# Linear attention and gated MLP, two layers: key weights folded on TensorE for all tiles, and a new order of instructions

## Chip, cores, metric

One core of one Trainium2 chip. The metric is the device time of one execution in microseconds (us), median of several runs. Ratios are the mean time of one kernel's fast runs over that of the kernel before in the same rounds, with a 95% interval; so they are not quite the ratio of the medians quoted beside them.

## The reference, cut to what matters

The input has 2048 rows of 512 (bf16). Two layers, each an attention block and an MLP block, each on a layer-normalised copy with a residual sum. There are 32 heads of 16 features.

```
qkv   = x @ wqkv
pq,pk = per head:  q @ w_phi[h],  k @ w_phi[h]
phi   = concat(softmax(p), softmax(-p))          # for q and k: "two signs"
kv    = sum over all rows of phi_k^T v ;  z = sum over all rows of phi_k
o     = (phi_q @ kv) / (phi_q @ z + 1e-6) ;      x += o @ wo
mlp:    x += (relu(x @ W_gate) * (x @ W_up)) @ W_down
```

The sum over all rows is a barrier: no query product with `kv` can start before the last tile of 128 rows has given its keys.

## The kernel before, the parts that matter

The program makes some 2,100 operations, each for one engine, with a priority (`DUE`), and plans one order from them. Some operations can run on two engines; a string of bits (`PLACE`) chooses. The planned order is then emitted once, so each engine executes a fixed sequence.

The key projection and w_phi are folded into one weight, Wk2 = wk @ blockdiag(w_phi). For that wk must be transposed. Before, the DMA transposes it from HBM, and because that comes late, tiles 0 and 1 take a detour ("unfolded": project, copy, multiply by the block-diagonal).

```python
def fold(w, dst, loaded, due, step, engs, by_dma=False):
    wT = Buf(p_wT)
    for m in range(NB):                       # NB = 4 blocks
        if by_dma:
            ... nc.sync.dma_start_transpose(out=wT..., in_=w[m*P:(m+1)*P, :])   # "wT"
            continue
        ps = Buf(p_b)                         # this branch was there, unused
        tr = op("PE", ... 4 x nc.tensor.matmul(ps..., lhsT=w[:, m, b*P:(b+1)*P], rhs=ident) ...)   # "turn"
        turned.append(evac(engs[m % 2], ... ps -> wT ...))
    for m in range(NB):
        f = op("PE", ... 4 x matmul(ps..., lhsT=wT.t[:, b, m*P:(m+1)*P], rhs=Wblk[:, b, :]) ...)   # "fold"
        done.append(evac(engs[m % 2], ... ps -> dst[:, m, :] ...))                                 # "W2"
...
k_fold = fold(A_wqkv[:, D:2 * D], Wk2, None, 10, 3000, ("ACT", "DVE"), True)
q_fold = fold(A_wqkv[:, 0:D], Wq2, None, ..., ("ACT", "DVE"), True)
...
# per tile t, layer 0 and 1 (cut):
k  = K products (4 matmuls of 512 columns), or keys_unfolded for t < UNFOLDED
ek = exp(+k), exp(-k)                                    # ScalarE, 2 x 512 columns
v  = V products, copied to vext                          # ScalarE or VectorE
sk = sum of each head of ek                              # VectorE, 1024 columns
lnk, rk = ln(sk), exp(-ln)                               # ScalarE
phi = ek * rk                                            # two halves, GpSimd or VectorE
kvz: sums += phi^T [v, 1]                                # TensorE
...
# after the last tile: R = block-diagonal of the sums, sign by sign (VectorE), then the query products
```

The softmax here doesn't subtract the row's maximum and nothing guards it: scores larger than these inputs give would overflow.

## Time and profile before

| | kernel before |
|---|---|
| median of 6 runs | 387.62 us (387.31 to 388.71) |
| span in the profile | 385.5 us, granted clock 1.000 |
| first folded key product | 16.86 us |
| first block-diagonal sum R | 55.27 us |
| first MLP product | 66.84 us |
| TensorE busy, of it fillers up to 15.1 us | 374.3 us, 6.26 us |

How to read it: up to R the kernel makes keys and values for 16 tiles and fits the queries in; this I call the key phase. From R on TensorE is busy nearly without a gap to the end. So the time of R and of the first MLP product tell whether the start got shorter, and the rest can be compared on its own. Two rows of instruction groups on VectorE, from the start of the kernel before to 54.9 us, become important later (columns: group, count, busy us, mean ns of one, idle before):

```profile
L665 DVE TENSOR_SCALAR xn<-X,mvA,rsA 128x512 bf16<-128x512 bf16 x16 | 6.7, 441 | 0.6 <-ACT rsA L660 0.6
L722 DVE TENSOR_TENSOR phiK<-ek,sk 128x512 bf16<-128x512 bf16 x9 | 6.6, 772 | 0.0
```

### The profile page before, as it was taken

What the parts mean: (1) busy time and instruction counts of PE and PEld (TensorE: products, weight loads), DVE (VectorE), ACT (ScalarE), POOL (GpSimd) and SP (SyncE); (2) the same over time, 40 slices, a digit from 0 to 9 for tenths busy, and PEclk for the clock granted to TensorE, in tenths of its full rate; (3) what the DMA queues carried; (4) which work ended last, traced back from release to release, by engine and by line L of the source; (5) the groups of instructions that cost most, each with busy time, mean ns of one, the idle gap of its engine ahead of it and who ended that gap; (6) DMA issues with size and microseconds to landing.
All of it is one profiled execution on the core that took longest, in us unless ns stands there. A gap on an engine that the chain in (4) does not pass through costs nothing.

```text
span 385.5 us, 7662 instructions
## 1 busy us (share of the span) xinstructions
PE 374.3 (97%) x2811; PEld 225.8 (59%) x2857; DVE 312.8 (81%) x793; ACT 216.5 (56%) x555; POOL 39.4 (10%) x42
## 2 busy tenths in 40 slices
PE   8999998999999999999999999999999999999996
PEld 3545455877655544455667645596774445445875
DVE  5999999999999988557985697999997699663434
ACT  4899999645457536256365489983345412421421
POOL 0266820000010203010012201000000000000000
PEclk9999999999999999999999999999999999999999
DMA  9787640143224141011101000014234023211110
GB/s 233 113 248 209 166 131 2 37 70 62 43 55 70 27 84 27 14 30 34 29 14 36 15 1 0 3 32 66 56 70 98 14 42 83 41 16 61 32 32 27
DMA packets 63046, 23.36 MB, mean 61 GB/s; under 512 B 54849, under 2 KB 61985, under 8 KB 63009
## 3 DMA queue, kind: packets, MB, share of 16 engines
q1 hardware_dynamic: 62592, 22.48, 26.6%
q8 instruction: 22, 0.36, 0.4%
q10 hardware_dynamic: 416, 0.39, 0.4%
q14 instruction: 16, 0.12, 0.1%
HBM read 7.91 MB, written 2.10 MB: 26 GB/s over the span
## 4 chain that ended last, share of the span: by engine, by line
PE 71%; DVE 17%; ACT 5%; DMA 3%; issue 3%; SPq 0%; DVEq 0%; ACTq 0%
PE b L894 31%; PE b L927 18%; PE b L830 5%; PE b L780 4%; PE b L698 4%; PE b L692 3%; PE q L798 3%; DVE sk L703 2%; PE b L870 2%; DVE bstA L650 2%; DMA xnTA<-xn 2%; PE q L739 1%; DVE xn L665 1%; DMA X<-in_A_x_dram 1%; DVE hT L902 1%
## 5 line engine op out<-in xcount | busy, mean ns | idle before, releaser
L894 PE MATMUL b<-xnTB,wgu 128*128 128x128 bf16 (+2 forms) x1192 | 152.0, 279 | 1.2 <-ACT xnTB L590 0.8
L894 PEld LDWEIGHTS <-wgu 128*128 128x128 bf16 x1200 | 98.0, 98 | 45.6 <-issue 1.0
L898 ACT ACTIVATE gu<-b 128x512 bf16<-128x512 f32 (+1 forms) x83 | 48.0, 583 | 66.4 <-PE b L894 62.8
L927 PE MATMUL b<-wd,hT 128*128 128x512 bf16 (+2 forms) x347 | 84.4, 372 | 0.9
L722 POOL TENSOR_TENSOR phiK<-ek,sk 128x512 bf16<-128x512 bf16 x36 | 38.7, 1094 | 192.8 <-ACT sk L713 121.7
L902 DVE TENSOR_TENSOR hT<-gu 128x512 bf16<-128x512 bf16 (+1 forms) x83 | 34.6, 417 | 24.9 <-ACT gu L590 23.9
L927 PEld LDWEIGHTS <-hT 128*128 128x128 bf16 (+1 forms) x363 | 34.0, 98 | 31.8 <-DVE hT L902 1.1
L695 ACT ACTIVATE ek<-b 128x512 bf16<-128x512 f32 x64 | 36.1, 607 | 10.3 <-PE b L692 10.3
L703 DVE TENSOR_REDUCE sk<-ek 128x64 f32<-128x1024 bf16 x32 | 38.5, 1209 | 3.7 <-ACT ek L695 3.4
L590 ACT CAST gu<-b 128x512 bf16<-128x512 f32 (+1 forms) x51 | 29.1, 570 | 20.0 <-PE b L894 19.7
L784 ACT ACTIVATE Eq<-b 128x512 bf16<-128x512 f32 x64 | 36.3, 631 | 0.4 <-PE b L780 0.2
L934 DVE SCALAR_TENSOR_TENSOR X<-b,rsB,X 128x512 bf16<-128x512 f32 (+1 forms) x33 | 23.6, 727 | 11.6 <-PE b L927 11.4
L830 PE MATMUL b<-wo,oT 128*128 128x512 bf16 x121 | 32.2, 379 | 0.7 <-ACT oT L590 0.2
L698 PE MATMUL b<-wv,xnTA 128*128 128x512 bf16 x125 | 32.0, 379 | 0.2
L590 ACT CAST N<-q 128x384 bf16<-128x384 f32 (+1 forms) x58 | 25.0, 452 | 12.2 <-PE q L798 10.6
L780 PE MATMUL b<-xnTA,Wq 128*128 128x512 bf16 x124 | 31.1, 379 | 0.2
L692 PE MATMUL b<-Wk,xnTA 128*128 128x512 bf16 x114 | 29.8, 379 | 0.7 <-DMA xnTA<-xn 0.4
L798 PE MATMUL q<-R,Eq 128*128 128x144 bf16 x256 | 27.7, 226 | 0.7 <-DVE R L761 0.3
L591 DVE CAST gu<-b 128x512 bf16<-128x512 f32 (+1 forms) x32 | 21.5, 676 | 7.7 <-PE b L894 7.5
L798 PEld LDWEIGHTS <-Eq 128*128 128x128 bf16 x256 | 20.2, 98 | 10.3 <-issue 2.1
L650 DVE BATCH_NORM_STATS2 bstA<-X 128x6 f32<-128x512 bf16 x32 | 21.4, 684 | 3.4 <-DMA X<-in_A_x_dram 3.2
L834 DVE TENSOR_TENSOR X<-X,b 128x512 bf16<-128x512 bf16 x32 | 21.6, 676 | 2.0 <-PE b L830 2.0
(70 smaller groups left out, 395.5 us busy)
## 6 DMA issues: line engine op xcount, KB each, us to landing
out_dram<-X SPq DMA_DIRECT2D x15, 128.0 KB, 1.7
X<-in_A_x_dram SPq DMA_DIRECT2D x6, 256.0 KB, 3.7
wgu<-in_B_W_gate_dram SPq DMA_DIRECT2D x4, 344.0 KB, 4.0
wgu<-in_B_W_up_dram SPq DMA_DIRECT2D x4, 344.0 KB, 3.5
wd<-in_B_W_down_dram SPq DMA_DIRECT2D x5, 256.0 KB, 3.9
wv<-in_A_wqkv_dram SPq DMA_DIRECT2D x2, 256.0 KB, 5.0
wo<-in_A_wo_dram SPq DMA_DIRECT2D x4, 128.0 KB, 2.8
oT<-o SPq DMA_TRANSPOSE x28, 2.4
```

Of the source, the lines that this page charges most:

```text
L590: both = {"ACT": ("ACT", act(cols), lambda: nc.scalar.copy(out=out_(), in_=in_()), False), "DVE": ("DVE", dve(cols), lambda: nc.vector.ten ...
L692: k = op("PE", mm(4, 512), due, lambda: [nc.tensor.matmul(kp.t[:], lhsT=xnTA[c][:, b, cols], rhs=Wk2[:, b, :], start=(b == 0), stop=(b == ...
L698: v = op("PE", mm(4, 512), due_v, lambda: [nc.tensor.matmul(vp.t[:], lhsT=xnTA[c][:, b, cols], rhs=wv[:, b, :], start=(b == 0), stop=(b == ...
L703: a = op("DVE", SUM16, due, lambda: nc.vector.tensor_reduce(out=sk.t[:, row, :], in_=ek.t[:].rearrange("p g s (h f) -> p (g s h) f", f=DH) ...
L722: e.tensor_tensor(out=ph.t[:].rearrange("p g s (h f) -> p (g s h) f", f=DH)[:, lo:lo + n], in0=ek.t[:].rearrange("p g s (h f) -> p (g s h) ...
L780: q = op("PE", mm(4, 512), due(c, b), lambda b=b, qp=qp: [nc.tensor.matmul(qp.t[:], lhsT=Wq2[:, m, b * P:(b + 1) * P], rhs=xnTA[c][:, m, : ...
L798: pe.append(op("PE", mm(len(groups), GE), due, lambda ps=ps, groups=groups: [nc.tensor.matmul(ps.t[:, n * GE:(n + 1) * GE], lhsT=Eq[c][:, ...
L830: a = op("PE", mm(4, 512), due + 3, lambda: [nc.tensor.matmul(yp.t[:], lhsT=oT.t[:, b, :], rhs=wo[:, b, :], start=(b == 0), stop=(b == NB ...
L894: nc.tensor.matmul(ps.t[:, q * W:(q + 1) * W], lhsT=wgu[:, s, b, g * P:(g + 1) * P], rhs=xT.t[:, b, 0:W], start=(b == 0), stop=(b == NB - 1))
L898: nc.scalar.activation(out=gu.t[:, 0, 0:cols], in_=gp.t[:, 0:cols], func=AF.Relu)
L902: nc.vector.tensor_tensor(out=h.t[:, f0 * W:f0 * W + cols], in0=gu.t[:, 0, 0:cols], in1=gu.t[:, 1, 0:cols], op=Alu.mult)
L927: nc.tensor.matmul(yp.t[:, 0:c1 - c0], lhsT=h.t[:m, f * W + i * P:f * W + (i + 1) * P], rhs=wd[:m, f, c0:c1], start=(f == 0), stop=(f == N ...
```

## The change

Intent: have the folded keys earlier by turning wk on TensorE, from the copy that is on chip anyway, and drop the detour. Priorities and placement are new for the whole program.

```diff
-UNFOLDED = 2
-PLACE = ( ... 299 bits ... )        DUE = ( ... 2105 priorities ... )
+PLACE = ( ... 301 bits ... )        DUE = ( ... 2105 priorities ... )
-    k_fold = fold(A_wqkv[:, D:2 * D], Wk2, None, 10, 3000, ("ACT", "DVE"), True)
-    def keys_unfolded(t, kp, xT, due):
-        ... 16 matmuls of 128 columns, a copy, 4 matmuls of 128 columns ...
+    k_fold = fold(wk, Wk2, l_wk, 100, 100, ("ACT", "DVE"))
...
-            if self.l == 0 and t < UNFOLDED:
-                k = keys_unfolded(t, kp, xT, due)
-            else:
-                k = op("PE", mm(4, 512), due, ... K products with Wk2 ...)
+            k = op("PE", mm(4, 512), due, ... K products with Wk2 ...)
```

## The prediction

> **What bounds the kernel now.** I read the page first, then the busy time of each engine in stretches, then the first 20 us in order of time, and the chain of waits last. The page's first part:
>
> ```profile
> PE 374.3 (97%) x2811; PEld 225.8 (59%) x2857; DVE 312.8 (81%) x793; ACT 216.5 (56%) x555; POOL 39.4 (10%) x42
> ```
>
> TensorE is busy for 97% of a 385.5 us span, so any gain has to come from time in which it is idle or does work that the result doesn't need. Fillers (matmuls on a tile of zeros, line 584) are such work. The stretches show where both lie; columns are the stretch, its length, then busy us and instruction count of each engine:
>
> ```profile
> 0.00:6.00 6.00, 4.13 (x16) 1.65 (x17) 3.26 (x16) 1.86 (x4) 0.70 (x6) 1.00 0.69 199
> 6.00:15.10 9.10, 8.27 (x82) 5.03 (x82) 7.31 (x20) 6.50 (x19) 0.00 (x0) 1.00 0.93 201
> 15.10:57.00 41.90, 41.16 (x312) 21.20 (x315) 40.57 (x70) 39.85 (x109) 24.59 (x23) 1.00 0.71 181
> 57.00:67.00 10.00, 8.50 (x69) 5.02 (x70) 9.16 (x30) 9.99 (x31) 0.00 (x0) 1.00 0.01 2
> 240.00:251.00 11.00, 10.24 (x84) 6.16 (x84) 10.08 (x33) 10.75 (x31) 0.00 (x0) 1.00 0.01 2
> 251.00:380.00 129.00, 128.21 (x1004) 82.02 (x1017) 95.34 (x274) 49.12 (x112) 0.00 (x0) 1.00 0.23 48
> ```
>
> The reader is to see four things. In the first 15.1 us TensorE looks busy, but 3.90 + 2.36 = 6.26 us of its 12.40 us are fillers (same stretches, filler line alone). From 15.1 to 57 us, the keys and values of layer 0 with the queries fitted in, TensorE (41.2 of 41.9), VectorE (40.6) and ScalarE (39.9) are all full; only GpSimd has room (24.6). At 57 to 67 and 240 to 251 us, where attention begins in each layer, TensorE loses 1.5 and 0.8 us. Elsewhere it loses under 1%.
>
> Why is so little real work done before 15 us? The folded key weights come late:
>
> ```profile
> 5.32 10.94 SPq L600 DMA_TRANSPOSE hT<-in_A_wqkv_dram  x8
> 10.99 1.07 ACT L590 CAST Wk<-b 128x512 bf16<-128x512 f32 x2
> 12.98 0.67 DVE L591 CAST Wk<-b 128x512 bf16<-128x512 f32 x1
> 16.33 0.67 DVE L591 CAST Wk<-b 128x512 bf16<-128x512 f32 x1
> 16.37 1.19 SPq L638 DMA_TRANSPOSE xnTA<-xn  x1
> 16.86 1.03 PE L692 MATMUL b<-Wk,xnTA 128*128 128x512 bf16 x4
> ```
>
> Eight weight transposes (four for keys, four for queries) hold the issuing queue from 5.32 to 16.26 us; the fourth block of folded keys is copied at 16.33 us, and the first folded key product runs at 16.86. The detour for tiles 0 and 1 bridges this. Of the chain to 62 us, 10.7% is the key sum (VectorE, line 703), 10.0% the waits for transposes of activations, 8.4% query products: no single engine, but VectorE comes first.
>
> **What the Trainium skill says.** "DMA: Bandwidth & Descriptors", section "Alternative transpose paths", lists TensorE as the way to transpose data that is already on chip, with an identity, from SBUF into PSUM. That fits: the weight wk is on chip anyway. "TensorE: Matmul & The Clock Gate", Part 4, adds the price, a copy out of PSUM afterwards. The kernel here uses plain matmuls on the identity; the trace has four of them in 0.40 us (line 641) and the copy in about 0.59 us on ScalarE or 0.68 us on VectorE. "VectorE: DVE Perf Modes", section "Why PSUM operands drop a tier", says that an fp32 operand in PSUM holds VectorE to its single-rate mode; the trace agrees, since a 512-column copy out of PSUM takes 685 ns against 415 ns for the 512-column SBUF sum of line 826. So each added turn costs more on the copying engine than on TensorE. The main skill page, "Trainium Kernel Development and Optimization", section "Best Practices", warns not to judge the distance to roofline by matmul busy time; the 6.26 us of fillers are a case of it.
>
> **The change, part by part.** The short description names attention sums built sign by sign; the diff doesn't touch that code, which already loops over signs in the kernel before, so it is worth 0. Three parts remain.
>
> *Key fold on TensorE.* Removed: four DMA transposes of about 1.27 us of queue time each, 5.1 us in all. Added: 16 matmuls of 128 columns, 4 x 0.22 = 0.9 us of TensorE, and four copies of 0.6 to 0.7 us, 2.5 us together. When are folded keys ready? The two halves of wk were issued at 0.7 and 1.2 us with 3.4 and 3.7 us to landing: 4.1 and 4.9 us. The turns can follow at once. The block-diagonal w_phi is ready at 5.34 + 0.69 = 6.03 us. Four folds and four copies on two engines, beside the first xn copy, take about 2.3 us: complete near 8.3 us, an estimate, against 16.95 us now. That is 8.6 us earlier, and the queue is 5.1 us freer for tiles 4 and up.
>
> *No unfolded keys.* Removed: 32 matmuls of 128 columns (16 in about 0.87 us at the pace of the trace, so 1.7), 8 more (0.4), two ScalarE copies (1.2). Added: 8 matmuls of 512 columns (2 x 0.86 = 1.7). TensorE over both parts: +0.9 + 1.7 - 2.1 = +0.5 us, no saving. Tile 0 gets its keys at about the same time (8.3 now), but tile 1, whose exponentials now start at 15.57 us, and tiles 2 and 3 can go as soon as their x is there (7.8 to 9.8 us).
>
> *New placement string and order.* These come with the diff and re-decide the whole order. I matched the placement bits to the operations in the order in which the program makes them; for the kernel before this gives nine VectorE and 23 GpSimd phi halves in layer 0, as the trace has them. The new string gives, in the key phase of layer 0: VectorE two turn copies more (+1.4), one fold copy less (-0.7), one value copy less (-0.7), two phi halves more (+1.4): +1.4 us. ScalarE: two turn copies, one fold copy and one value copy more, two copies less: +1.2 us. GpSimd two halves less.
>
> **The sum.** TensorE alone could gain much: before 15.1 us it does 12.40 - 6.26 = 6.1 us of real work now and could do about 9.5 (turns and folds 1.7, four tiles of K and V 6.9, turns of xn 0.9), 3.4 us more, less the 0.5 added: 2.9 us. But the keys must also pass VectorE, which is full from 7.8 us on. Its work there changes by -1.4 (two key-fold copies, one of them gone, the other early) - 0.7 (value copy) + 1.4 (phi) = -0.7 us; the two turn copies fit into its hole between 6.03 and 7.82 us. Its holes later, 0.24, 0.51 and 0.44 us, can close in part. So the sums R, begun at 55.27 us now, should begin 0.7 to 1.9 us earlier, about 1.3. TensorE, ahead with its queries by then, waits for that. As it is bound from there on, this carries to the end nearly whole. I add 0.4 us for idle time that a new order may take off the two attention starts (2.3 us in all): 387.55 - 1.3 - 0.4 = 385.85, said as 385.8 us.
>
> **The rivals.** *TensorE sets the start, and the gain is the 2.9 us or more.* For it: it is full from 15.1 us on and its lead is real; ScalarE is idle for over 3 us between 5 and 15 us and could take VectorE's work. Against: the new string gives VectorE more, not less. Time: about 384. *The start is hidden and nothing comes of it.* VectorE has the same keys to sum (16 x 1.2 us), a new copy falls on the statistics of tiles 1 to 3, and TensorE merely idles later, near 55 us, instead of filling early. For it: VectorE at 40.6 of 41.9 us. Against: the small holes that do go away. Time: 387 to 388. *The new order hurts elsewhere.* The new string moves six of the 512-column copies of the up-projection and four value copies of layer 1 from ScalarE to VectorE in layer 0's main part, where VectorE is full in 100 to 130 us already. Against: it has slack from 140 to 240 us, and three phi halves go the other way. Time: 388 to 390.
>
> **Range and chances.** The work of TensorE hardly changes, and all that isn't its needed work is the 6 us of fillers and some 8 us of idle time up to 380 us, so over 2% (7.75 us, under 379.8) would need most of that: 0.03. Slower by over 2% needs a new wait of 8 us in a tuned order: 0.02. Within 2%: 0.95. The first rival's 384 with some luck gives the low end, 383.5; a wash with a slightly worse order the high end, 387.9.
>
> **What would show it right or wrong.** In the changed profile: four weight transposes instead of eight, and 16 matmuls with wk before 6 us; folded keys complete at 8 to 9 us and a first line of their product by 9.5 us, not 16.9; fewer fillers than the 6.3 us now; more real TensorE work before 15 us by 2 to 4 us; VectorE still full from about 8 us to the first R, and this R 0.7 to 1.9 us earlier; from R to the end the same length within 1 us. I am wrong in the mechanism if R comes 3 us earlier (VectorE was no bound), if it doesn't move while TensorE idles more before it, or if the difference arises after 67 us, where I have only the new order to blame.

## The result and the profile after

The changed kernel takes 386.5 us (386.07 to 386.79, 6 runs) against 387.62 us; ratio 0.9967 (0.9954 to 0.9981). That is 1.1 us faster, a real but small gain, within 2%.

The same stretches of the changed kernel (columns as in the prediction: stretch, length, busy us and count of TensorE, its weight loads, VectorE, ScalarE, GpSimd; then clock, DMA share, GB/s):

```profile
0.00:6.00 6.00, 4.74 (x21) 2.54 (x22) 3.45 (x17) 2.37 (x4) 0.70 (x6) 1.00 0.75 207
6.00:15.10 9.10, 8.48 (x76) 5.44 (x74) 8.66 (x20) 7.74 (x21) 0.00 (x0) 1.00 0.60 155
15.10:57.00 41.90, 41.54 (x307) 21.09 (x306) 40.41 (x74) 40.23 (x110) 22.66 (x21) 1.00 0.70 177
57.00:67.00 10.00, 8.36 (x84) 5.37 (x82) 9.45 (x31) 9.29 (x30) 0.00 (x0) 1.00 0.01 2
...
251.00:380.00 129.00, 128.94 (x1009) 81.61 (x1007) 93.59 (x270) 49.44 (x116) 0.00 (x0) 1.00 0.22 48
```

VectorE does 8.66 us of work between 6 and 15.1 us, against 7.31 before, and ScalarE 7.74 against 6.50. Fillers are 3.60 + 1.76 us there, so TensorE's real work before 15.1 us is 13.22 - 5.36 = 7.9 us against 6.1: 1.7 us more. Not all of that is a lead. By 15.1 us both kernels have done the values and keys of two tiles; the changed one has done 16 more fold matmuls (32 against 16) and 4 more turns of xn, about 1.1 us at 0.056 us each (an estimate from the pace of the trace). The rest is mostly the new turns of wk. In order of time, the fold of the changed kernel:

```profile
4.27 2.61 SPq L600 DMA_TRANSPOSE hT<-in_A_wqkv_dram  x2
...
4.65 1.06 PE L605 MATMUL b<-ident,hT 128*128 128x128 bf16 x8
...
5.86 1.44 DVE L591 CAST hT<-b 128x512 bf16<-128x512 f32 x2
...
8.95 1.08 ACT L590 CAST Wk<-b 128x512 bf16<-128x512 f32 x2
...
9.80 1.03 PE L676 MATMUL b<-Wk,xnTA 128*128 128x512 bf16 x4
```

Four weight transposes are left (two here, two from 7.56 us, all for the queries). The turns of wk run from 4.65 to 7.0 us, VectorE makes its two turn copies from 5.86 us, and the first folded key product runs at 9.80 us instead of 16.86.

The first sums R on VectorE, kernel before and then changed kernel:

```profile
55.27 0.42 DVE L761 TENSOR_TENSOR R<-q,Mf 64x256 bf16<-64x256 f32 x1 [0.44 <-PE q L739]
```

```profile
53.53 0.55 DVE L751 SCALAR_TENSOR_TENSOR R<-q,Mf 64x16 bf16<-64x16 f32 x3 [0.36 <-PE q L723]
```

R begins 1.74 us earlier; its first large sum, of 64 x 256 as in the line before, begins at 54.09 us. The first query product with it runs at 55.51 us (56.97 before, 1.46 earlier), the first MLP product at 65.63 us (66.84, 1.21 earlier), the span ends at 384.4 us (385.5, 1.1 earlier). So the whole gain lies before R: from the first MLP product to the end both kernels take the same, 385.5 - 66.84 = 318.7 and 384.4 - 65.63 = 318.8 us. Between R and the first MLP product the changed kernel loses half a microsecond, the larger part of it (0.28 us) before the first query product: its new order builds three of the small denominators before the first large sum.

Where does R's 1.7 us come from? VectorE's stretches up to the end of its last phi, kernel before and then changed kernel:

```profile
0.00:7.82 7.82, 5.93 (x35) 2.86 (x36) 3.29 (x17) 2.54 (x5) 0.70 (x6) 1.00 0.78 237
7.82:54.83 47.01, 45.50 (x353) 23.95 (x359) 46.20 (x80) 43.56 (x121) 24.59 (x23) 1.00 0.77 186
```

```profile
0.00:7.82 7.82, 6.56 (x38) 4.14 (x39) 4.83 (x19) 3.74 (x7) 0.70 (x6) 1.00 0.86 227
7.82:53.17 45.35, 44.63 (x337) 22.98 (x336) 44.68 (x80) 43.11 (x121) 22.66 (x21) 1.00 0.72 183
```

VectorE is busy for the same total, 3.29 + 46.20 = 49.5 and 4.83 + 44.68 = 49.5 us, but it ends 1.66 us earlier, and 4.83 - 3.29 = 1.54 us more of it is done before 7.82 us. This is a balance of times, not yet a cause. In the kernel before VectorE waits there for x:

```profile
5.34 0.69 DVE L573 TENSOR_TENSOR Wblk<-wf,Mf 128x512 bf16<-128x512 bf16 x1
7.82 1.29 DVE L650 BATCH_NORM_STATS2 bstA<-X 128x6 f32<-128x512 bf16 x2 [1.79 <-DMA X<-in_A_x_dram]
```

Part of this hole is chance: in four more profiled runs of the same structure (below) these statistics start at 7.08 to 7.41 us.

TensorE gives a second account. From 12.6 us to R it has no idle time over 0.1 us in the changed kernel:

```profile
12.60:53.50 40.90, 40.81 (x307) 20.89 (x307) 39.90 (x68) 39.12 (x110) 22.66 (x21) 1.00 0.72 182
```

In the kernel before it waits once from 11 us to R, 0.4 us near 47.5 us, for a transpose of activations. What it still has to do differs: after 12.4 us it runs 24 fold matmuls before R in the kernel before and 4 in the changed kernel. Those 20 are about 1.1 us of R's 1.74 (an estimate at 0.056 us each).

One thing I had not foreseen: the new string gives VectorE more operations, yet its busy time is the same. The same two group rows of the changed kernel, up to 53.3 us:

```profile
L706 DVE TENSOR_TENSOR phiK<-ek,sk 128x512 bf16<-128x512 bf16 x11 | 7.0, 676 | 0.0
L652 DVE TENSOR_SCALAR xn<-X,mvA,rsA 128x512 bf16<-128x512 bf16 x16 | 6.1, 399 | 0.6 <-ACT rsA L647 0.6
```

A phi takes 676 ns on average against 772 before, an xn 399 against 441. That is 9 x 96 + 16 x 42 ns = 1.5 us, as much as the added operations cost. The experiments show what this is.

### The profile page after: what moved, and what is told of

The parts are those of the page before. It is cut to its first block, busy times and chain, and to the rows that moved or that the text cites. A ratio compares the mean times of both kernels' runs of the same rounds, so it can differ in the third digit from the quotient of the medians.

```text
span 384.4 us, 7669 instructions
## 1 busy us (share of the span) xinstructions
PE 375.9 (98%) x2834; PEld 226.1 (59%) x2834; DVE 316.6 (82%) x804; ACT 211.1 (55%) x545; POOL 40.6 (11%) x43
## 4 chain that ended last, share of the span: by engine, by line
PE 84%; DVE 12%; issue 2%; ACT 1%; DVEq 0%
PE b L878 33%; PE b L911 17%; PE b L676 7%; PE b L682 7%; PE b L814 5%; PE b L764 5%; PE q L782 3%; PE b L854 3%; PE q L723 2%; DVE bstB L637 1%; DVE hT L886 1%; PE q L584 1%; DVE bstA L637 1%; DVE pr L807 1%; DVE gu L591 1%
## 5 line engine op out<-in xcount | busy, mean ns | idle before, releaser
L911 PE MATMUL b<-wd,hT 128*128 128x512 bf16 (+2 forms) x363 | 85.9, 373 | 0.0
L706 POOL TENSOR_TENSOR phiK<-ek,sk 128x512 bf16<-128x512 bf16 x37 | 39.9, 1101 | 193.2 <-ACT sk L697 190.7
L679 ACT ACTIVATE ek<-b 128x512 bf16<-128x512 f32 x64 | 35.4, 604 | 16.6 <-PE b L676 16.5
L918 DVE SCALAR_TENSOR_TENSOR X<-b,rsB,X 128x512 bf16<-128x512 f32 (+1 forms) x33 | 23.6, 724 | 11.8 <-PE b L911 11.6
L590 ACT CAST gu<-b 128x512 bf16<-128x512 f32 (+1 forms) x42 | 24.4, 581 | 16.2 <-PE b L878 16.1
L590 ACT CAST N<-q 128x384 bf16<-128x384 f32 (+1 forms) x60 | 26.9, 464 | 11.3 <-PE q L782 8.5
L676 PE MATMUL b<-Wk,xnTA 128*128 128x512 bf16 x128 | 32.4, 379 | 0.1
L591 DVE CAST gu<-b 128x512 bf16<-128x512 f32 (+1 forms) x41 | 26.4, 646 | 6.7 <-PE b L878 6.5
```

The lines of the kernel that those rows point to most:

```text
L590: both = {"ACT": ("ACT", act(cols), lambda: nc.scalar.copy(out=out_(), in_=in_()), False), "DVE": ("DVE", dve(cols), lambda: nc.vector.ten ...
L676: k = op("PE", mm(4, 512), due, lambda: [nc.tensor.matmul(kp.t[:], lhsT=xnTA[c][:, b, cols], rhs=Wk2[:, b, :], start=(b == 0), stop=(b == ...
L706: e.tensor_tensor(out=ph.t[:].rearrange("p g s (h f) -> p (g s h) f", f=DH)[:, lo:lo + n], in0=ek.t[:].rearrange("p g s (h f) -> p (g s h) ...
L911: nc.tensor.matmul(yp.t[:, 0:c1 - c0], lhsT=h.t[:m, f * W + i * P:f * W + (i + 1) * P], rhs=wd[:m, f, c0:c1], start=(f == 0), stop=(f == N ...
```

## The experiments

Theory: VectorE sets the time of R, and the change gains by filling its early hole. Rivals: TensorE's lead sets R; the new order alone is the gain; the fillers matter; stretched VectorE instructions in the kernel before were the cost. "Order frozen" means that the plan is made as before and only what an operation emits is altered, so each engine's sequence stays. The time of R and the span are those of one profiled execution. Spans of one kernel scatter (384.3 to 385.0 us in six executions of the changed kernel, 385.1 to 386.7 in nine of the kernel before), so a few tenths of R mean something only where the trace shows what made them. With the order frozen one can follow, operation by operation, how far each engine is ahead of or behind the run that it is compared with.

| run | R, us | span | median | ratio to before (interval) |
|---|---|---|---|---|
| kernel before | 55.27 | 385.5 | 387.62 | 1 |
| changed kernel | 53.53 | 384.4 | 386.50 | 0.9967 (0.9954, 0.9981) |
| sum_half | 53.11 | 384.0 | 385.45 | 0.9954 (0.9940, 0.9968) |
| kv_three | 54.44 | 386.0 | 388.41 | 1.0025 (1.0011, 1.0038) |
| both_less | 52.22 | 383.8 | 385.64 | 0.9962 (0.9949, 0.9974) |
| no_fill | 53.73 | 384.6 | 386.40 | 0.9974 (0.9961, 0.9986) |
| before_vec_hole | 55.08 | 385.0 | 387.13 | 0.9981 (0.9949, 1.0014) |
| before_vec_late | 57.82 | 387.8 | 389.31 | 1.0037 (1.0005, 1.0070) |
| before_pe_late | 56.29 | 386.6 | 388.47 | 1.0015 (0.9981, 1.0049) |
| before_pool_half | 54.61 | 384.9 | 387.44 | 0.9990 (0.9958, 1.0021) |
| new_code_old_order | 58.04 | 389.7 | 391.36 | 1.0115 (1.0101, 1.0129) |
| old_code_new_order | 60.40 | 393.1 | 394.20 | 1.0186 (1.0169, 1.0203) |
| after_vec_hole | 54.50 | 385.6 | 387.34 | 1.0003 (0.9987, 1.0019) |
| after_pool_half | 54.03 | 384.9 | 386.10 | 0.9971 (0.9949, 0.9993) |

### First four: take work away in the changed kernel

sum_half, the key sums of layer 0 read half of each head (a wrong computation, though the result stays within the tolerance, as the scale largely cancels between numerator and denominator):

```diff
-  in_=ek.t[:].rearrange("p g s (h f) -> p (g s h) f", f=DH)
+  in_=ek.t[:].rearrange("p g s (h f) -> p (g s h) f", f=DH)[:, :, 0:DH // 2 if self.l == 0 else DH]
```

> The changed kernel with its order frozen, but the 16 key sums of layer 0 read only half of each head (wrong result on purpose). That takes about 0.5 us off VectorE for each tile, some 8.5 us in the key phase, and nothing off any other engine. VectorE sets the start (my theory): the first sum R (53.5 us in the changed kernel) comes at least 1.5 us earlier and the kernel ends at least 1.2 us earlier, under 385.3 us. TensorE's lead sets the start (first rival): R moves by less than 0.5 us and the end by less than 0.5 us, 386.0 to 386.6 us.

kv_three, one of four blocks left out of K and V in layer 0 (wrong result), both_less with both edits:

```diff
+  nk = NB - 1 if self.l == 0 else NB
-  stop=(b == NB - 1)) for b in range(NB)]
+  stop=(b == nk - 1)) for b in range(nk)]
```

> The changed kernel with its order frozen, but the key and value products of layer 0 leave out one of four blocks (wrong result on purpose). That takes 32 matmuls of 0.216 us, 6.9 us, off TensorE in the key phase and nothing off VectorE. VectorE sets the start: R moves by less than 0.7 us, TensorE idles 5 us or more before it, and the end by less than 1 us, above 385.5 us. TensorE's lead sets the start: R comes 3 us earlier or more, the end 3 to 6.9 us earlier, 379.5 to 383.5 us.

> Both edits together, order frozen (wrong result on purpose): 8.5 us less on VectorE and 6.9 us less on TensorE in the key phase. VectorE alone sets the start: the same R and end as with the half sums alone, within 0.5 us. If two engines hold each other up in turn, the two savings together give clearly more than the sum of the single ones: R 3 us earlier or more. ScalarE, 40 of 42 us busy in the key phase, keeps the gain under 5 us in any case.

no_fill, no fillers after the first eight:

```diff
-  free, filling = None, True
+  free, filling = None, False
```

> The changed kernel without the fillers that the order puts in after the first eight (6 to 8 of them, about 1.8 us between 6 and 15 us, right result). If they are idle time in disguise, as the prediction counts them: R and end within 0.4 us of the changed kernel, 386.1 to 386.9 us. If they keep the granted clock up: the clock in the records drops below full before 15 us, matmuls there take longer, R and the end come 0.5 to 3 us later.

*What was measured.* Taking 8.5 us off VectorE (16 sums of 678 instead of 1208 ns) left R only 0.42 us earlier, where my theory wanted 1.5. Even these 0.42 us aren't the sums': TensorE's first value product, at 6.87 instead of 7.40 us, was 0.53 us early before the first key sum had run. The median, 385.45 us, lies between the two forecasts (under 385.3, or 386.0 to 386.6). Its row for 15.1 to 57 us tells why R stayed; the row of kv_three follows:

```profile
15.10:57.00 41.90, 41.52 (x307) 21.14 (x306) 34.12 (x74) 40.16 (x111) 21.92 (x21) 1.00 0.72 177
```

```profile
15.10:57.00 41.90, 36.45 (x269) 17.90 (x270) 41.00 (x73) 39.24 (x109) 22.30 (x21) 1.00 0.68 177
```

VectorE falls to 34.12 us, but TensorE is full at 41.52, and from 12.2 us to R it waits once, 0.1 us. So in the changed kernel R follows TensorE, not VectorE. In kv_three TensorE has 5 us of room, VectorE is full at 41.00 us, and R comes 0.9 us *later*. With less work and the same sequence, something must have become slower, and the records show it. VectorE and GpSimd of kv_three:

```profile
19.92 1.06 POOL L707 TENSOR_TENSOR phiK<-ek,sk 128x512 bf16<-128x512 bf16 x1 [1.88 <-ACT sk L698]
...
19.98 1.14 DVE L652 TENSOR_SCALAR xn<-X,mvA,rsA 128x512 bf16<-128x512 bf16 x1
...
22.15 1.05 POOL L707 TENSOR_TENSOR phiK<-ek,sk 128x512 bf16<-128x512 bf16 x1 [1.18 <-ACT sk L698]
...
22.32 1.43 DVE L707 TENSOR_TENSOR phiK<-ek,sk 128x512 bf16<-128x512 bf16 x1
```

The xn on VectorE starts 0.06 us after a phi on GpSimd and takes 1.14 us, not 0.40: it ends 0.14 us after GpSimd's phi does. The phi at 22.32 us takes 1.43 instead of 0.68. The Trainium skill names this: "SBUF — State Buffer", section "SBUF: two separate sides", says that VectorE and GpSimd share one port pair, an exclusive lock for a whole instruction, taken by a VectorE instruction in a two-port mode or with two SBUF inputs, and whoever starts first has it. The trace agrees; the key sums (one input, 1.2 us each) are never stretched. In kv_three two such collisions cost 1.5 us of VectorE (0.74 + 0.75), which it passes on to R in part (VectorE has next to no other idle time there; the link to R is argued from that). The changed kernel has the same sequence, but there the xn comes first and GpSimd does the waiting, 1.24 instead of 1.06 us:

```profile
20.27 0.40 DVE L652 TENSOR_SCALAR xn<-X,mvA,rsA 128x512 bf16<-128x512 bf16 x1
...
20.35 1.24 POOL L706 TENSOR_TENSOR phiK<-ek,sk 128x512 bf16<-128x512 bf16 x1 [1.89 <-ACT sk L697]
```

A shift by some tenths of a microsecond decides which of the two loses. The kernel before has the same kind of collision in an xn of 0.92 us and a phi of 1.52 us; these are its higher means above. sum_half and both_less have such collisions too: their longer xn and phi add about 1.0 and 2.2 us to VectorE, which has idle time there.

both_less moved R by 1.31 us, more than the two single runs together (-0.42 + 0.91). That fits two engines that hold each other up, but doesn't show it: the 0.91 comes from two collisions, and in both_less TensorE also waits 1.9 us for transposes of activations. It stayed far from the 3 us that I had allowed for that case.

no_fill has R and span within 0.2 us of the changed kernel, and the granted clock stayed full: the fillers that the order adds are idle time in disguise, as the prediction counted them. (The first eight stay in every run; what they do wasn't tested.) It shows something else as well. Its first folded key product came at 9.01 us, 0.79 us earlier, and VectorE ran about half a microsecond ahead of the changed kernel from 7.7 to 39 us. Yet R came 0.20 us later, since TensorE had to wait for a transpose of activations:

```profile
33.73 1.04 PE L676 MATMUL b<-Wk,xnTA 128*128 128x512 bf16 x4 [0.59 <-DMA xnTA<-xn]
```

From there TensorE is 0.20 us behind the changed kernel up to R. VectorE loses its lead after 39 us and ends 0.20 us late too. In this run an earlier start of VectorE doesn't reach R.

### Next four: add work to the kernel before

before_vec_hole and before_vec_late, the same two spare reductions at two places; before_pe_late; before_pool_half (wrong result):

```diff
  for o in order:
+     if o is first_K: idle(6)                                  # before_pe_late only
      o.emit()
+     if o.name == "Wblk":      # before_vec_hole;   before_vec_late: behind the key sum of tile 4
+         for _ in range(2): nc.vector.tensor_reduce(out=spare, in_=zero (64 groups of 8), op=add)
  def phi(e, lo, n):
+     if e is nc.gpsimd and self.l == 0: n = n // 2             # before_pool_half, phi tiles preset once by GpSimd
```

> The kernel before with its order frozen and two spare reductions of 0.6 us each (1.2 us, result unused) put on VectorE right behind the block-diagonal w_phi, where it waits from 6.03 to 7.82 us. The hole is free (my theory: the two turn copies of the change cost nothing there): the first R stays at 55.3 us within 0.3, the end within 0.4 us of the kernel before. If work anywhere on VectorE counts: R and end 1.2 us later.

> The same two spare reductions, 1.2 us, put on VectorE behind the key sum of tile 4 (near 20 us) instead. VectorE sets the start: R and end 0.8 to 1.4 us later. TensorE or ScalarE sets it: R and end within 0.4 us.

> The kernel before, order frozen, six more matmuls of 512 columns on zeros (1.3 us of TensorE, result unused) ahead of the first folded key product at 16.9 us. VectorE sets the start and TensorE only follows: R and end within 0.5 us of the kernel before. TensorE is as critical as VectorE: R and end 0.9 to 1.4 us later. The half sums in the changed kernel moved R by 0.4 us only, so I now lean to between the two.

> The kernel before, order frozen, each GpSimd phi of layer 0 made half as long, the other half constant (wrong result on purpose). In the kernel before one xn took 0.92 us instead of 0.40 and one phi 1.52 instead of 0.68 on VectorE while GpSimd ran a phi; in the changed kernel none did. If those stretches cost the kernel before its 1.1 us: they vanish, VectorE's busy time up to R falls by 1 us or more, R comes 1 to 1.7 us earlier and the time falls to about 386.4. If they don't matter (other holes take their place): R moves under 0.5 us and the time stays at 387.2 to 387.7 us.

*What was measured.* The rounds scattered more (the kernel before 386.49 to 390.96 us), so the intervals only exclude large effects. One line of TensorE and one of VectorE in before_vec_hole, then one of TensorE in before_vec_late:

```profile
16.69 0.40 PE L614 MATMUL b<-Wblk,hT 128*128 128x128 bf16 x4 [0.78 <-DMA hT<-in_A_wqkv_dram]
17.42 0.69 DVE L592 CAST xnTA<-b 128x512 bf16<-128x512 f32 x1 [0.87 <-PE b L642]
```

```profile
36.97 1.04 PE L693 MATMUL b<-Wk,xnTA 128*128 128x512 bf16 x4 [1.25 <-DMA xnTA<-xn]
```

In the hole the 1.2 us don't delay R (0.19 us earlier), but this run can't say that the hole alone made them free. The statistics came 0.6 us earlier than in the kernel before (7.22 us), and this lead was lost at 16.6 us: a weight transpose for the queries landed late, TensorE waited for it ahead of the first folded key product, and VectorE waited for TensorE. So VectorE ran 0.3 to 0.5 us late from there to 49 us. R is early because after that a phi, 1.52 us in the kernel before, wasn't stretched. What holds is that early VectorE time is cheap in this structure. In all four runs of it with edits TensorE waits for that transpose (the sixth of eight), which landed at 16.1 to 16.7 us, and VectorE then waits 0.3 to 0.9 us. In the profiled run of the kernel before it landed at 14.7 us and nothing waited; in the changed kernel, where four are left, the last landed at 11.7. That the shorter queue is part of the gain is likely by this, but no run tests it alone.

At 26 us, where the order puts that key sum, the same 1.2 us delay R by 2.55 us, more than they last: an xn right behind them now takes 1.26 us, the lock again, and TensorE waits 1.31 us for an exponential and 1.25 us for a transpose of activations. So the place decides, as the theory says. 1.3 us more of TensorE delays R by 1.02 us; I had said under 0.5 if TensorE only follows, 0.9 or more if it is as critical. It is at least as critical. Shorter GpSimd instructions bring R 0.66 us earlier, not the 1 to 1.7 that the stretches would have given if they were the whole cost. In this run the presetting itself collided with VectorE (a small copy at 2.10 us took 1.04 instead of 0.20), inside the time that VectorE waits anyway. The lock can be a part of the kernel before's cost, not all of it; 0.66 us is near the scatter of single executions.

### Two that carry code and order over to each other

Each operation that both kernels have got its planned start in one kernel as its priority in the other; the turns got the priorities of the weight transposes and the reverse.

> The changed structure (keys folded on TensorE, no unfolded keys) with the order and placement of the kernel before: each operation that both have keeps its planned start as its priority; the turns take those of the weight transposes. Right result. If the structure is the gain and the order adds little: R near 53.5 us, time 386 to 387 us. If structure and order only work together: R 2 us or more later than in either kernel, 57 to 58 us, time 389.5 to 391.5 us.

> The structure of the kernel before (weight transposes by DMA, two unfolded tiles) with the order and placement of the changed kernel, carried over in the same way. Right result. If the new order is the gain and the structure adds nothing: R near 53.5 us, time 386 to 387 us. If structure and order only work together: R 57 to 59 us, time 389.5 to 392 us. From R to the end it should take as long as the changed kernel, within 0.5 us, since that part of the order is the same.

*What was measured.* Both are slower than either kernel, by 4.4 us and 7.3 us against the kernel before's 386.94 us of these rounds. R comes at 58.0 and 60.4 us. So neither part has a gain of its own that could be read off: an order is fitted to one set of operations, and any other set in it loses more than the change is worth. From R to the end old_code_new_order took 393.1 - 60.4 = 332.7 us, not the changed kernel's 330.9 that I expected; its granted clock fell to 0.96 in the stretch from 57 to 67 us, which the changed kernel's did not. new_code_old_order took 331.7 us from R, against 330.3 in the kernel before, with a clock of 0.92 in that stretch. Why the clock fell wasn't tested. A version with only one part, tuned as long as these two were, was not tried and stays open.

### Two mirror runs in the changed kernel

The same edits as before_vec_hole and before_pool_half, now in the changed kernel.

> The changed kernel, order frozen, with the same two spare reductions (1.2 us of VectorE, result unused) at the same place as in the kernel before: right behind the block-diagonal w_phi. There they were free in the kernel before. If the change lives on filling that hole, the hole is gone now: folded keys, first R and end come 0.7 to 1.3 us later, which gives back most of the 1.1 us, 387.1 to 387.9 us. If the hole has nothing to do with the gain: R and end within 0.3 us of the changed kernel, 386.2 to 386.8 us.

> The changed kernel, order frozen, each GpSimd phi of layer 0 half as long (wrong result on purpose). Here no xn or phi on VectorE is stretched, so there is little to win: R moves by under 0.4 us (0.66 us in the kernel before). If R comes 0.7 us or more earlier, it was GpSimd's own time and not the stretching that counted in both.

*What was measured.* after_vec_hole puts its 1.2 us behind the block-diagonal w_phi again, and VectorE's order of time reads:

```profile
5.72 1.40 DVE L1003 TENSOR_REDUCE spare<-zero 128x64 f32<-128x512 bf16 x2
7.03 1.28 DVE L592 CAST hT<-b 128x512 bf16<-128x512 f32 x2
8.28 0.69 DVE L592 CAST Wk<-b 128x512 bf16<-128x512 f32 x1
8.88 1.28 DVE L638 BATCH_NORM_STATS2 bstA<-X 128x6 f32<-128x512 bf16 x2
```

The turn copies slide to 7.03 us, the statistics of tile 1 from 8.28 to 8.88, the first folded key product from 9.80 to 10.41, R from 53.53 to 54.50, and the time is 387.34 us, ratio 1.0003: the whole gain is given back. It reaches R by way of TensorE, which waits for the second turn copy:

```profile
7.77 0.40 PE L614 MATMUL b<-Wblk,hT 128*128 128x128 bf16 x4 [1.42 <-DVE hT L592]
```

Of the 0.97 us, TensorE is 0.61 behind at once; the rest comes between 33 and 36 us. What cost nothing in the kernel before costs everything in the changed one: work there delays the folded keys. after_pool_half is spoiled: the presetting by GpSimd held a VectorE copy from 2.21 us for 2.72 us and the first statistics behind it, so the first xn starts 0.8 us late, the first folded key product 0.4, and R is 0.50 us later; under 0.4 was expected. Its xn and phi take 400 and 679 ns as in the changed kernel, so there was no stretch to remove, but the claim about R is neither shown nor refuted.

No experiment gave a valid version that is clearly faster than the changed kernel (sum_half computes something else; no_fill is valid and the same).

## Why the prediction was right

Predicted 385.8 us (383.5 to 387.9), measured 386.5. The range holds the kernel before's own 387.6 too, so a hit on it says little; the steps say more.

- *Folded keys earlier.* Right in kind, 1 us too early: complete at 10.0 us (8.3 estimated; it was 17.0 before by the line shown, not 16.95), first product at 9.80 (9.5 at most; its record starts before the last copy ends), turns done at 7.0 (before 6). The working also misread why the keys were late before: the trace has the four key transposes landed by 12.35 us and the fourth fold run at 13.80; its copy came at 16.33 because VectorE's order put other work first. From 5.3 to 10 us ScalarE makes two turn copies, three fold copies, the first xn copy and a value copy one after the other; the value copy I had left out, and each copy waits for its matmuls. The pace of TensorE is the other part: in the profiled run the 16 turns start 0.107 us apart, not 0.055, since TensorE came to its full pace only at 7.1 us; in no_fill it had it at about 4 us, and the product came at 9.01. That moment lies between about 4 and 7.2 us in the profiled runs, and the granted clock that the profile gives reads 1.00 before and after it.
- *TensorE, 3.4 us more real work before 15 us.* Measured 1.7, of which 1.1 is a lead (estimate above). Keys and values of four tiles were expected by then and two were done, as before; the new order runs the query folds there instead.
- *VectorE, and R 0.7 to 1.9 us earlier.* Measured 1.74, near the upper end, but not by the path that the working gave. The hole was its main term. Useless work there costs 0.97 us of R in the changed kernel, through TensorE, and none in the kernel before, where other waits hide it. The working had one term too few: stretched instructions, 1.5 us in the kernel before and none on VectorE after, which cancelled the work that the new string adds. That the two cancel is luck.
- *"VectorE comes first" as the bound, and TensorE waits for it.* This step failed for the changed kernel. Relieved of 8.5 us, VectorE gives at most 0.42 us; TensorE has no idle time over 0.1 us from 12.6 us to R; and in no_fill R follows TensorE, with VectorE ahead up to 39 us. VectorE is close behind: with less work for TensorE (kv_three) it is full at 41.00 us and R comes later. In the kernel before, 1.3 us more on TensorE costs 1.02 us. The change gave both an earlier start, VectorE 1.54 us and TensorE about 1.1 us (20 folds out of the full stretch). The traces favour TensorE's; no run separates the two, so this split stays open.
- *"This carries to the end nearly whole" and 0.4 us more at the attention starts.* The term of 0.4 us was wrong in sign: R to the first MLP product takes 12.1 us instead of 11.6. So 1.74 became 1.2, and 1.1 at the end. Against the working, the R term came out 0.4 us larger and the attention term 0.9 us smaller; with 0.1 us in the rest, the gain is 1.1 us and not 1.7.
- *Rivals.* TensorE sets the start, 2.9 us or more (384): the size is refuted, the mechanism is nearer to the traces than the one that I chose. Nothing comes of it (387 to 388): no. The new order hurts elsewhere: no, 318.7 and 318.8 us from the first MLP product on.

## What to carry to other kernels

When three engines are each 95% busy, one of them relieved gives little (8.5 us off VectorE gave at most 0.42 us here). With a frozen order, follow each engine's lead over the run that you compare with: the engine whose lead or lag lasts up to the end point is the one to shorten. Look for a stretch where the fullest ones wait together, usually at the start, and move work there. Test such a hole directly: put useless work in it and see whether the end moves, and check in the trace that no later wait hid it. And an order that was tuned with the code can't be judged apart from it: a correct small change in a foreign order lost 4 to 7 us here, and in kv_three the same sequence lost about 1 us, most likely by instructions of VectorE and GpSimd meeting.

## What the Trainium skill lacked or had wrong

- "TensorE: Matmul & The Clock Gate", section "Back-to-back issue gap", gives sustained spacings in a stream with weight loads of about 81 ns at 128 columns and 131 ns at 512, and says that 216 ns at 512 over-counts. Here four 512-column matmuls with their weight loads repeat every 0.86 us, 215 ns each, and 16 matmuls of 128 columns take 0.9 us, 56 ns each. So the figures that the page gives for a single matmul fit this stream, and the sustained ones don't. The starts in the changed kernel:

```profile
40.10 1.02 PE L676 MATMUL b<-Wk,xnTA 128*128 128x512 bf16 x4
40.96 1.03 PE L682 MATMUL b<-wv,xnTA 128*128 128x512 bf16 x4
41.82 1.03 PE L676 MATMUL b<-Wk,xnTA 128*128 128x512 bf16 x4
```

- "SBUF — State Buffer", section "SBUF: two separate sides": right that the loser waits for the whole instruction; the section doesn't say how this looks in a profile. The wait is inside the duration of the VectorE instruction (0.40 became 1.14 us, 0.68 became 1.43), so it counts as busy and shows in no list of waits; compare the mean of a group with its shortest. When GpSimd loses, it is GpSimd's record that grows (1.06 to 1.24 us).
- "DMA: Bandwidth & Descriptors", section "DMA Transpose (X-bar)": I found no figure there for how long one transpose of 128 x 512 bf16 holds its issuing queue (another page has a time for 128 x 128, without saying what of it is the queue's). In the kernel before it is 1.19 to 1.32 us for activations, and 1.22 to 1.74, median 1.27, for the eight of the weights, which took 10.94 us together; so a queue of them delays what is issued behind.
